# An mLSTM cell feeding a quick-GELU layer: the second chunk's gates computed later, one batch's mask moved to GpSimd, ScalarE's conversion steps separated, and the loads put in another order

## The chip, the core and the metric

The kernel runs on one core of one Trainium2 chip. The metric is the device time of one execution in microseconds, the median of several runs; less is better. Five runs of the kernel before gave 485.58, 485.70, 485.89, 485.89 and 486.21 us.

A core has engines that run beside each other, each on its own list of instructions in a fixed order: TensorE (PE in the profile; its weight loads are shown as PEld), VectorE (DVE), ScalarE (ACT), GpSimd (POOL), and SyncE (SP), which here only issues DMAs. An instruction starts when the one before it on its engine has gone ahead and the semaphores it waits for have come.

## What is computed

Two layers, one behind the other. The first is a recurrent cell over 768 steps for 4 batches of 8 heads, head size 40; the second multiplies each of the 3072 rows of 320 numbers by a 320 x 2048 matrix, applies a quick GELU, and multiplies by a 2048 x 320 matrix.

```python
for t in range(S):
    m_new = np.maximum(f_gate[:, :, t] + m, i_gate[:, :, t])
    f_stab = np.exp(f_gate[:, :, t] + m - m_new)
    i_stab = np.exp(i_gate[:, :, t] - m_new)
    m = m_new
    C = f_stab[..., None, None] * C + i_stab[..., None, None] * np.einsum('bhd,bhe->bhde', vt, kt)
    n = f_stab[..., None] * n + i_stab[..., None] * kt
    h_tilde = np.einsum('bhde,bhe->bhd', C, qt)
    denom = np.maximum(np.abs(np.einsum('bhd,bhd->bh', n, qt)[:, :, None]), 1.0)
    y[:, :, t] = 1.0 / (1.0 + np.exp(-o_gate[:, :, t])) * h_tilde / denom
...
h = x @ w_in
out = (h * (1.0 / (1.0 + np.exp(-1.702 * h)))) @ w_out
```

## The kernel before

The 768 steps are cut into six chunks (`w` = 0 to 5) of 128 steps. Within a chunk the recurrence becomes an attention: scores k times q (`scores`, L350), multiplied on VectorE by a matrix of decay weights that is zero above the diagonal (`weights`, then L352), times v (`values`, L362), divided and gated on VectorE (`y`, L389 to L395), transposed (`seam`, L404 on TensorE, L405 on ScalarE) and given to the up projection, the GELU and the down projection. What a chunk hands on is a state per head.

The gates of a chunk are two scans and six short operations on VectorE (`gates`, L254 to L281), on 32 partitions (one per batch and head). The running maximum `m_run` is also written to DRAM as a row (L269), from where `spread` (L316) reads it back, broadcast over 128 partitions, as the raw material of the next chunk's weights. For chunks from 1 on, ScalarE turns these into weights with eight activations per batch (L334), and GpSimd sets what lies above the diagonal to zero (L336). Chunk 0 has no time for the way through DRAM: there TensorE builds the exponents in PSUM from bf16 parts (L328, L329). A first matmul (L324) puts -1e30 above the diagonal, so that ScalarE's exponential (L330) gives zero there.

The weights of both projections come from DRAM in twenty pieces of 512 KB: 0 to 9 are `w_in`, 10 to 19 are `w_out`. `fetch` issues the loads, `convert` turns a piece into the form that TensorE uses: two ScalarE steps (L228 on the high words into the destination, L229 on the low words in place) and four VectorE steps (L232, L233, L235, L237), of which only L237 reads what L229 wrote. Six pieces fit into the tile `big`, and a slot is free again when its piece has been converted: piece 10 takes the slot of piece 0, and so on.

There is no scheduler: each engine's order is the order in which the program writes the calls (`manual_schedule`). SyncE issues nearly all DMAs in one order as well: at the start gates, keys and queries (`"kq"`), values and output gates (`"vo"`) by batch, and the weight pieces in between. An issue that has to wait holds what follows. For chunk 1 the keys and queries are also loaded as blocks of 32 steps (`load_blocks`, 16 DMAs each for `k_bl` and `q_bl`, L117), which VectorE transposes (L301). PSUM has eight tiles; `ps_a` has four of them in turn, so a matmul may also wait until an earlier reader of its tile is done.

Chunk 0 starts with a list written out by hand (L683 to L740). Then comes the loop over chunks: `up` or `up_fast`, then the down projection in blocks. In chunk 0 the function `weights_in(n)` places the conversions between the stages from a table `beside`, with the fetches that go with each; the pieces of the next chunk's attention (`side`) are put between the down blocks.

Of the kernel before, what the change touches and what calls it, by code (L numbers as in the profile page):

```python
# [12 lines left out]
OP = mybir.AluOpType  # L13
# [9 lines left out]
L = 128  # L23
# [11 lines left out]
def kernel(  # L35
# [13 lines left out]
    B, H, S, D = q.shape  # L49
# [4 lines left out]
    NP = H // 2  # L54
# [20 lines left out]
    V, A, G, T = nc.vector, nc.scalar, nc.gpsimd, nc.tensor  # L75
# [91 lines left out]


    load_gates(0)
    for what, n in (("kq", 0), ("kq", 1), (load_gates, 1), ("vo", 0), ("vo", 1), ("kq", 2), (fetch, 0), ("kq", 3),  # L170
                    (fetch, 1), ("vo", 2), ("vo", 3), *((fetch, n) for n in range(2, 10))):
        if isinstance(what, str):
            load(0, what, slice(n, n + 1))
        else:
            what(n)
# [5 lines left out]
    not_yet, ident_bf = (xs.bitcast(BF)[:, i * L:(i + 1) * L] for i in range(2))  # L181
# [21 lines left out]
    for t in (k_st, q_st):  # L203
# [16 lines left out]
    kT, qT, wt, ys, xT, gs, o_ps, p_c = {}, {}, {}, {}, {}, {}, {}, {}  # L220


    def convert(n, engines="AV"):

        lo, hi, dst = bits[n][:, :, 0], bits[n][:, :, 1], pieces[n][0]
        dst_u = dst.bitcast(U32)
        if "A" in engines:
            A.activation(out=dst, in_=hi.bitcast(FP), func=AF.Abs)  # L228
            A.activation(out=lo, in_=lo, func=AF.Copy, scale=2.0 ** -29)  # L229
        if "V" not in engines:  # L230
# [81 lines left out]
    def spread(w):  # L312

        for b in range(B):
            x = wt[w, b] = work.tile([L, NP, 2, L], FP, tag="wt", bufs=4, name="wt")
            nc.sync.dma_start(out=x.rearrange("s p i t -> s (p i) t"),  # L316
                              in_=m_row[w][b * H:(b + 1) * H, :].unsqueeze(0).to_broadcast([L, H, L]))

    def weights(w, b):
        if w == 0:  # L320
            x = wt[w, b] = work.tile([L, NP, 2, L], FP, tag="wt", bufs=4, name="wt")
            for i in range(2):
                pw = ps_a.tile([L, NP, L], FP, tag="a", name="p_w")
                T.matmul(pw, ident_bf, not_yet.unsqueeze(1).to_broadcast([L, NP, L]), start=True, stop=False)  # L324
                for p in range(NP):
                    h = b * H + 2 * p + i
                    one = pick[:, h:h + 1].to_broadcast([3 * BH, L])
                    T.matmul(pw[:, p, :], one, m3, start=False, stop=False)  # L328
                    T.matmul(pw[:, p, :], a3, one, start=False, stop=(p == NP - 1))  # L329
                A.activation(out=x[:, :, i, :], in_=pw, func=AF.Exp)  # L330
            return
        x = wt[w, b].rearrange("s p i t -> s (p i) t")
        for h in range(H):
            A.activation(out=x[:, h, :], in_=x[:, h, :], func=AF.Exp, scale=-1.0,  # L334
                         bias=cols[w][:, b * H + h:b * H + h + 1])
        G.affine_select(out=x, in_=x, compare_op=OP.is_ge, fill=0.0, base=0, pattern=[[0, H], [1, L]],  # L336
                        channel_multiplier=-1)
        if w > 1 and b == 0:
            gates_out(w)

# [342 lines left out]
    transposes(0, 0)  # L683
    weights(0, 0)
    transposes(0, 1)
    gates(1)
    scores(0, 0)
    weights(0, 1)
    scores(0, 1)
# [2 lines left out]
    values(0, 0)  # L692
    values(0, 1)
    transposes(0, 2)
    convert(0, "A")
    weights(0, 2)
    seam(0, 0)
    seam(0, 1)
    convert(0, "V")
    scores(0, 2)  # L700
    convert(1, "A")
    transposes(0, 3)
    weights(0, 3)
    convert(1, "V")
    scores(0, 3)
# [17 lines left out]
    values(0, 3, states=True)  # L723
    full_rows(0, 0, 0)
    full_rows(1, 0, 0)
    convert(2, "A")
    seam(0, 2)
    full_rows(0, 1, 0)
    seam(0, 3)
# [7 lines left out]
    for j in range(2):  # L737
        for i in range(2):
# [2 lines left out]

    beside = {0: ((5,), range(10, 15)), 1: ((6, 7, 8), ()), 2: ((9, 10, 11), (16,)), 3: ((12, 13, 14), (18, 19)),
              4: ((15,), ()), 8: ((16,), ()), 10: ((17,), ()), 12: ((18,), ()), 14: ((19,), ())}

    def weights_in(n):
        done, ahead = beside.get(n, ((), ()))
        for p in done:
            convert(p)  # L750
        for p in ahead:
            fetch(p)

# [7 lines left out]
    for w in range(NW):  # L761
        more = w + 1 < NW
        for j in range(NF // 2):
# [10 lines left out]
                up_fast(w, j, next_keys if more and j == 0 else None)  # L774
            if w == 0 and j == 0:
                load_blocks(1, 0)
                fetch(15)
                spread(1)
                load_blocks(1, 1)
            if w == 1 and j == 3:  # L780
                weight_sums(3)
            if more:
# [87 lines left out]
```

## Time and profile before

| what | value |
|---|---|
| median of five runs | 485.89 us (485.58 to 486.21) |
| the profiled execution's own time | 485.58 us |
| its span in the profile | 483.9 us |
| TensorE busy / weight loads busy | 478.0 us / 396.9 us |
| VectorE, ScalarE, GpSimd busy | 342.3, 220.9, 60.3 us |
| TensorE's granted clock | 1.00 over the span |
| DMA, mean over the span | 93 GB/s |
| DMA, second to fourth 12 us of the span | 210, 280, 286 GB/s |

The profile covers one execution; its span is a little shorter than the time, which also holds what lies before the first and after the last instruction. In lists of instructions the columns are start in us, duration in us, engine, line and operation, what it writes and reads, the count of instructions merged into the row, and in brackets how long the engine was idle before it and what ended the idle time. In the table of stretches each engine has its busy time and, in brackets, its number of instructions; behind them stand the granted clock, the busy share of the DMA engines and the GB/s.

### The profile page before, as it was taken

Reading aid. Unit: us, or ns where it says so; the run is one execution under the profiler, and the core shown is the slowest. Engines: PE = TensorE matmul, PEld = TensorE weight load, DVE = VectorE, ACT = ScalarE, POOL = GpSimd, SP = SyncE. Lnnn points to the kernel's source line nnn. Section 1 sums busy time; section 2 is a strip of 40 time slices with the busy share of each in tenths; the row PEclk is TensorE's granted clock in tenths of the full one; section 3 lists DMA queues with packets and bytes.
Section 4 is the critical chain, followed back from the end, with each engine's and each line's share of the span. In section 5 each row is a group of like instructions: output and inputs, shape, how many; then the busy total and the mean of one; then the engine's idle time right before and its main releaser. Section 6 shows DMA issues by size and latency. Waiting matters only on the chain. (4 is left out here: it accounts for less than half of the span.)

```text
span 483.9 us, 10433 instructions
## 1 busy us (share of the span) xinstructions
PE 478.0 (99%) x4072; PEld 396.9 (82%) x4072; DVE 342.3 (71%) x853; ACT 220.9 (46%) x575; POOL 60.3 (12%) x101
## 2 busy tenths in 40 slices
PE   8999999999999999999999999999999999999997
PEld 5874467777779999788999877999877999977997
DVE  8788888887978965667766677686576786254831
ACT  7667675403649302468600466900374920255300
POOL 3020001520001420000341000332000120000000
PEclk9999999999999999999999999999999999999999
DMA  9999779944997000997000896200492000000000
GB/s 127 210 280 286 165 140 235 133 65 72 193 177 79 6 30 28 218 152 81 3 29 15 126 249 65 28 28 3 85 261 21 1 15 16 28 1 0 1 34 22
DMA packets 176097, 44.87 MB, mean 93 GB/s; under 512 B 164368, under 2 KB 169648, under 8 KB 176048
## 3 DMA queue, kind: packets, MB, share of 16 engines
q1 hardware_dynamic: 175472, 43.55, 48.9%
q8 instruction: 32, 0.52, 0.5%
q10 hardware_dynamic: 576, 0.66, 0.4%
q14 instruction: 17, 0.14, 0.1%
HBM read 40.17 MB, written 4.01 MB: 91 GB/s over the span
## 5 line engine op out<-in xcount | busy, mean ns | idle before, releaser
L615 PE MATMUL p_out<-w_out_sb,g 128*128 128x160 f32 x480 | 69.8, 301 | 0.0
L615 PEld LDWEIGHTS p_out<-w_out_sb,g 128*128 128x128 f32 x480 | 66.3, 190 | 0.9
L405 ACT COPY xT<-p_x 128x384 f32<-128x384 f32 x24 | 10.8, 483 | 122.1 <-PE p_x L404 109.0
L526 DVE TENSOR_TENSOR g<-p_u,g 128x256 f32<-128x256 f32 x80 | 33.7, 424 | 44.6 <-PE p_u L518 35.0
L523 ACT COPY g<-p_u 128x256 f32<-128x256 f32 x120 | 43.1, 377 | 43.5 <-PE p_u L518 39.3
L530 ACT ACTIVATE g<-g 128x256 f32<-128x256 f32 x120 | 42.3, 425 | 39.3 <-DVE g L526 39.3
L336 POOL TENSOR_SCALAR_AFFINE_SELECT wt<-wt 128x1024 f32<-128x1024 f32 x20 | 22.7, 1137 | 238.0 <-ACT wt L334 208.1
L620 DVE TENSOR_TENSOR o_sb<-o_sb,p_out 128x160 f32<-128x160 f32 x70 | 21.4, 317 | 42.2 <-PE p_out L615 41.8
L334 ACT ACTIVATE wt<-wt,cols 128x128 f32<-128x128 f32 x160 | 47.8, 391 | 0.0
L518 PE MATMUL p_u<-xT,w_in_sb 128*128 128x256 f32 x160 | 38.9, 382 | 0.0
L518 PE MATMUL p_u<-xs,big 128*128 128x256 f32 x160 | 37.9, 379 | 0.0
L546 PE MATMUL p_v<-xT,w_in_x 64*128 64x512 f32 x80 | 37.0, 602 | 0.0
L546 PE MATMUL p_u<-xT,w_in_x 64*128 64x512 f32 x80 | 37.0, 602 | 0.0
L352 DVE TENSOR_TENSOR wt<-p_s,wt 128x512 f32<-128x512 f32 x48 | 30.4, 682 | 8.5 <-POOL wt L336 6.7
L566 PE MATMUL p_out<-w_out_sb,g 128*128 128x320 f32 x128 | 36.3, 436 | 0.0
L615 PE MATMUL p_out<-t,big 128*128 128x160 f32 x240 | 35.5, 301 | 0.0
L518 PEld LDWEIGHTS p_u<-xT,w_in_sb 128*128 128x128 f32 x160 | 29.6, 190 | 5.4 <-DVE o_sb L620 1.5
L518 PEld LDWEIGHTS p_u<-xs,big 128*128 128x128 f32 x160 | 30.0, 190 | 4.6 <-ACT g L523 0.2
L615 PEld LDWEIGHTS p_out<-t,big 128*128 128x128 f32 x240 | 33.3, 190 | 0.2
L566 PEld LDWEIGHTS p_out<-w_out_sb,g 128*128 128x128 f32 x128 | 23.8, 190 | 9.8 <-issue 0.5
L526 DVE TENSOR_TENSOR g<-p_v,g 128x256 f32<-128x256 f32 x80 | 29.8, 414 | 0.0
L546 PEld LDWEIGHTS p_v<-xT,w_in_x 64*128 64x128 f32 x80 | 14.2, 186 | 16.0 <-issue 16.0
(172 smaller groups left out, 857.3 us busy)
## 6 DMA issues: line engine op xcount, KB each, us to landing
wt<-m_row SPq DMA_DIRECT2D x20, 512.0 KB, 7.0
v_st<-in_v_dram SPq DMA_DIRECT2D x5, 640.0 KB, 8.8
eo<-in_o_gate_dram SPq DMA_DIRECT2D x5, 640.0 KB, 5.6
k_st<-in_k_dram SPq DMA_DIRECT2D x5, 640.0 KB, 11.2
out_dram<-o_sb SPq DMA_DIRECT2D x19, 160.0 KB, 1.8
big<-in_moe_w_in_dram SPq DMA_DIRECT2D x5, 512.0 KB, 6.6
k_bl<-in_k_dram SPq DMA_DIRECT2D x40, 64.0 KB, 2.7
q_bl<-in_q_dram SPq DMA_DIRECT2D x40, 64.0 KB, 2.6
```

The lines of the kernel that those rows point to most:

```text
L334: A.activation(out=x[:, h, :], in_=x[:, h, :], func=AF.Exp, scale=-1.0, bias=cols[w][:, b * H + h:b * H + h + 1])
L336: G.affine_select(out=x, in_=x, compare_op=OP.is_ge, fill=0.0, base=0, pattern=[[0, H], [1, L]], channel_multiplier=-1)
L352: V.tensor_tensor(out=wt[w, b][:, :, i, :], in0=pw[i], in1=wt[w, b][:, :, i, :], op=OP.mult)
L405: A.copy(out=xT[w][:, :, b, :], in_=px)
L518: T.matmul(p[k][:, ts[t]], a[:, k // 2, k % 2 * 128:(k % 2 + 1) * 128], b, start=first, stop=True, skip_group_check=True)
L523: A.copy(out=g[k][i][:, ts[t]], in_=chain[k][:, ts[0]])
L526: V.tensor_tensor(out=g[k][i][:, ts[t]], in0=p[k][:, ts[pt]], in1=g[k][i][:, ts[t]], op=OP.add)
L530: A.activation(out=dst, in_=dst if src is None else src, func=AF.Gelu_apprx_sigmoid)
L546: T.matmul(p[k], w_in_x[r, k, :], x[r, 2, :], start=False, stop=True, skip_group_check=True)
L566: T.matmul(po, gs[w, f // 2][:, f % 2, b * L:(b + 1) * L], w_out_sb[:, f, :], start=(f == 0), stop=(f == NF - 1))
L615: T.matmul(po, a(f), b[:, f, :], start=(f == 0), stop=(f == NH - 1))
L620: V.tensor_tensor(out=dst, in0=x, in1=po, op=OP.add)
```

## The change

Six edits, all of which concern chunk 0 and the material for chunk 1.

1. The loads of chunk 1's gates are issued behind the ten pieces of `w_in`, not behind the keys and queries of batch 1.
2. `gates(1)` leaves the list at the start, where it stood between the transposes of batch 1 and the scores of batch 0. It is called when piece 9 has been converted.
3. For batch 1 of chunk 0 the -1e30 matmul is left out (two instructions with their weight loads), and GpSimd sets the values above the diagonal to zero after the exponential, once for each half of the heads.
4. `convert` takes its ScalarE steps apart, "H" and "L". For piece 0, "L" comes behind the weights of batch 2; for piece 1, behind the transposes of batch 3.
5. In SyncE's order the blocks of keys come behind pieces 10 and 11, and the blocks of queries behind pieces 12 to 15. Before, keys stood behind pieces 10 to 14, and queries behind piece 15 and the broadcast.
6. The row's way through DRAM follows the gates: written behind the queries' blocks, read back (`spread(1)`) behind piece 16.

```diff
-    for what, n in (("kq", 0), ("kq", 1), (load_gates, 1), ("vo", 0), ("vo", 1), ("kq", 2), (fetch, 0), ("kq", 3),
-                    (fetch, 1), ("vo", 2), ("vo", 3), *((fetch, n) for n in range(2, 10))):
+    for what, n in (("kq", 0), ("kq", 1), ("vo", 0), ("vo", 1), ("kq", 2), (fetch, 0), ("kq", 3),
+                    (fetch, 1), ("vo", 2), ("vo", 3), *((fetch, n) for n in range(2, 10)), (load_gates, 1)):
...
-    def convert(n, engines="AV"):
+    def convert(n, steps="HLV"):
...
-        if "A" in engines:
+        if "H" in steps:
             A.activation(out=dst, in_=hi.bitcast(FP), func=AF.Abs)
+        if "L" in steps:
             A.activation(out=lo, in_=lo, func=AF.Copy, scale=2.0 ** -29)
...
+    def causal(x, n):
+
+        G.affine_select(out=x, in_=x, compare_op=OP.is_ge, fill=0.0, base=0, pattern=[[0, n], [1, L]],
+                        channel_multiplier=-1)
+
     def weights(w, b):
         if w == 0:
...
-                T.matmul(pw, ident_bf, not_yet.unsqueeze(1).to_broadcast([L, NP, L]), start=True, stop=False)
+                if b != 1:
+                    T.matmul(pw, ident_bf, not_yet.unsqueeze(1).to_broadcast([L, NP, L]), start=True, stop=False)
...
-                    T.matmul(pw[:, p, :], one, m3, start=False, stop=False)
-                    T.matmul(pw[:, p, :], a3, one, start=False, stop=(p == NP - 1))
+                    T.matmul(pw[:, p, :], one, m3, start=(b == 1), stop=False)
+                    T.matmul(pw[:, p, :], a3, one, start=False, stop=(b == 1 or p == NP - 1))
                 A.activation(out=x[:, :, i, :], in_=pw, func=AF.Exp)
+                if b == 1:
+                    causal(x[:, :, i, :], NP)
...
     transposes(0, 1)
-    gates(1)
     scores(0, 0)
...
-    convert(0, "A")
+    convert(0, "H")
     weights(0, 2)
+    convert(0, "L")
     seam(0, 0)
     seam(0, 1)
     convert(0, "V")
     scores(0, 2)
-    convert(1, "A")
+    convert(1, "H")
     transposes(0, 3)
+    convert(1, "L")
     weights(0, 3)
...
-    beside = {0: ((5,), range(10, 15)), 1: ((6, 7, 8), ()), 2: ((9, 10, 11), (16,)), 3: ((12, 13, 14), (18, 19)),
+    beside = {0: ((5,), (10, 11)), 1: ((6, 7, 8), ()), 2: ((9, 10, 11), (16,)), 3: ((12, 13, 14), (18, 19)),
...
             convert(p)
+            if p == 9:
+                gates(1)
...
             if w == 0 and j == 0:
                 load_blocks(1, 0)
-                fetch(15)
+                for n in range(12, 16):
+                    fetch(n)
+                load_blocks(1, 1)
+            if w == 0 and j == 4:
                 spread(1)
-                load_blocks(1, 1)
```

More of the change, by code (lines that the diff above doesn't have):

```diff
@@ L220 @@
     kT, qT, wt, ys, xT, gs, o_ps, p_c = {}, {}, {}, {}, {}, {}, {}, {}
-    def convert(n, engines="AV"):
+    def convert(n, steps="HLV"):
         lo, hi, dst = bits[n][:, :, 0], bits[n][:, :, 1], pieces[n][0]
         dst_u = dst.bitcast(U32)
-        if "A" in engines:
+        if "H" in steps:
             A.activation(out=dst, in_=hi.bitcast(FP), func=AF.Abs)
+        if "L" in steps:
             A.activation(out=lo, in_=lo, func=AF.Copy, scale=2.0 ** -29)
-        if "V" not in engines:
+        if "V" not in steps:
             return
@@ L335, in weights @@
                          bias=cols[w][:, b * H + h:b * H + h + 1])
-        G.affine_select(out=x, in_=x, compare_op=OP.is_ge, fill=0.0, base=0, pattern=[[0, H], [1, L]],
-                        channel_multiplier=-1)
+        causal(x, H)
         if w > 1 and b == 0:
@@ L725 @@
     full_rows(1, 0, 0)
-    convert(2, "A")
+    convert(2, "HL")
     seam(0, 2)
```

## The prediction

> **What bounds the kernel now.** I read the row of busy shares first, then the table by stretches of time, then VectorE's and TensorE's timelines of the first 30 us, then those of 50 to 85 us, where the moved work lands.
>
> ```profile
> PE 478.0 (99%) x4072; PEld 396.9 (82%) x4072; DVE 342.3 (71%) x853; ACT 220.9 (46%) x575; POOL 60.3 (12%) x101
> ...
> 8.00:26.50 18.50, 17.91 (x282) 15.24 (x279) 15.26 (x39) 12.14 (x26) 2.14 (x5) 1.00 1.18 210
> 26.50:36.20 9.70, 9.70 (x52) 7.21 (x48) 8.56 (x18) 6.51 (x11) 1.76 (x4) 1.00 1.02 279
> 36.20:66.50 30.30, 30.30 (x145) 13.69 (x144) 24.09 (x45) 20.66 (x37) 0.16 (x1) 1.00 0.84 224
> ```
>
> TensorE is busy 99%, at a granted clock of 1.00. A modelled end can hide a stall, so I checked its pace: 16 matmuls of the up stage take 7.13 us both at 43.15 and at 52.13, and 16 of L566 4.57 us at 85.50, 91.98 and 104.61. From 26.56 us on TensorE simply has work. A microsecond is won there only by less TensorE work, or by reaching 26.56 earlier, and then it stays won to the end. The start is different:
>
> ```profile
> 8.63 0.41 DVE L254 TENSOR_TENSOR_SCAN f_run<-one,fi 32x128 f32<-32x128 f32 x1 [0.48 <-DMA fi<-in_f_gate_dram]
> ...
> 10.82 0.22 DVE L281 TENSOR_SCALAR dec_in<-pair,both 32x16 f32<-32x16 f32 x1
> 10.97 1.27 DVE L352 TENSOR_TENSOR wt<-p_s,wt 128x512 f32<-128x512 f32 x2
> 13.35 1.29 DVE L352 TENSOR_TENSOR wt<-p_s,wt 128x512 f32<-128x512 f32 x2 [1.11 <-PE p_s L350]
> ...
> 12.29 0.96 PEld L350 LDWEIGHTS p_s<-qT,kT 40*128 40x128 f32 x14 [0.30 <-DVE wt L352]
> ...
> 19.08 0.29 PEld L350 LDWEIGHTS p_s<-qT,kT 40*128 40x128 f32 x2 [0.60 <-ACT wt L330]
> ...
> 25.62 0.90 PEld L362 LDWEIGHTS p_o<-v_st,wt 128*64 128x64 f32 x28 [0.15 <-DVE wt L352]
> ```
>
> VectorE starts the first scores' product (L352) at 10.97, right behind the eight instructions of gates(1) (8.63 to 11.04), though TensorE's scores ended at 9.08 + 1.16 = 10.24. TensorE then waits for L352 (11.69, 12.29), at 19.08 for ScalarE's L330, and at 25.62 again for VectorE.
>
> **The change, part by part.**
>
> *gates(1) out of the start.* L352 began 0.09 to 0.10 us before the modelled end of its scores at 13.35 and 20.63, so it can start at 10.14 instead of 10.97: **-0.83 us**. TensorE's second half of the next scores, held until the second L352 ended (12.24), starts near 11.46 and ends at 12.61 instead of 13.44: the 0.83 stays.
>
> *No mask matmul for batch 1.* Two matmuls L324, worth 0.23 and 0.21 us by the start of the next instruction (10.17 to 10.40, 10.85 to 11.06), leave TensorE. Without them TensorE is ready for the scores at 11.25, just before VectorE lets it go; with them it would be ready at 11.69 and eat 0.23 of the 0.83. They are part of that gain, not an addition.
>
> *Two masks on GpSimd, 128x512 each.* No such row. Nearest are 0.29 us for 128x128 (the start) and 1.09 for 128x1024 (L336); a line through them gives 0.65. Bounds: 0.55 (half of L336) and 1.09 each. ScalarE's two L330 would end at about 11.44 and 12.07, so the masks end at 12.16 and 12.81; the two L352 that need them start at 12.52 and 13.16. Hidden, with 0.35 to spare; at 1.09 each the second ends at 13.69 and costs 0.53.
>
> A rule speaks against this part. The Trainium skill, "SBUF — State Buffer", section "Who interferes with whom", has a VectorE instruction with two SBUF inputs and a GpSimd instruction that reads SBUF block each other for whole instructions. The trace agrees where the form fits: L494 (both inputs in SBUF) took 2.00 us at 72.03 beside the mask at 71.44, 1.18 us without it. But L352 reads its first input from PSUM:
>
> ```profile
> 158.90 1.09 POOL L336 TENSOR_SCALAR_AFFINE_SELECT wt<-wt 128x1024 f32<-128x1024 f32 x1 [1.25 <-ACT wt L334]
> ...
> 158.86 1.28 DVE L352 TENSOR_TENSOR wt<-p_s,wt 128x512 f32<-128x512 f32 x2
> ```
>
> Side by side, both keep their usual time. Were the lock to hold here, L352 would wait for 12.81 instead of 12.52: +0.29. I take the row: 0.
>
> *ScalarE's parts split.* L228 and L229 of piece 0 (17.29, 17.86) precede L330 (18.44), for which TensorE waits at 19.08. With L229 behind L330, L330 ends about 0.58 earlier, on top of the 0.83; these scores end near 19.3, no longer late. VectorE is then free at 20.44 - 0.83 = 19.61, and its 0.18 us wait before 20.63 goes: **-1.02** at the third batch's L352. L229 now ends at 18.88, its reader L237 starts at 18.92: hidden, barely. In the second split TensorE's transposes hold ScalarE's copies anyway: nothing.
>
> *What holds this back: loads.* Piece 1 of the weights was issued at 13.07 and landed after 7.2 us, at 20.27; its L228 ran at 20.30. If it lands no earlier, VectorE's conversion of piece 1 starts at 20.98 instead of 20.82 and the gain is 0.86. SyncE no longer issues two gate loads (4.57 to 5.81, 1.2 us) ahead of it, but the loads there land at a pace of 1.0 to 1.1 us each, so only some tenths can follow. Between 0.86 and 1.02 I take **-0.95**. The wait at 25.62 shows that TensorE passes this on.
>
> *gates(1) in its new place* follows piece 9's conversion on VectorE, near 50.1 us (51.08 - 0.95). Its eight instructions took 2.41 us from 8.63 to 11.04. Behind it wait the conversions of pieces 10 to 15. VectorE idled 1.26 us at 57.05 and 1.84 us at 66.04 for ScalarE, so piece 14 ends 2.41 - 1.26 = 1.15 late, at 64.40, and piece 15 on time. TensorE needs piece 14 first for f = 6, at 67.06 + 4 x 0.267 - 0.95 = 67.2. Cost 0; without those two pauses 2.41 would still fit into the 3.9 us by which piece 14 was early.
>
> *SyncE's queue.* Before: pieces 10 to 14 (to 42.62), keys' blocks (11.0 us), piece 15, the broadcast of m_row (54.73), queries' blocks (14.1 us, to 71.1), piece 16. After, from about 28.5: pieces 10 and 11 (2), keys (11.0), pieces 12 to 15 (4), queries (14.1), m_row (0.6) end near 60.2. Piece 12, issued near 42, lands after some 5 us, and ScalarE wants it at 55.4. Piece 16 comes about 10 us earlier and ends ScalarE's 1.60 us wait at 75.30, which TensorE never felt: 0.
>
> The broadcast becomes late: it waits for gates(1)'s row to land. Row: 1.4 us median for m_row; behind the queries' blocks 2.5 (their own landing). "DMA: Bandwidth & Descriptors", section on the anatomy of one DMA, puts a fixed part of about 2.0 us on any DMA, for GpSimd's path. By either the broadcast starts at 62.2 to 62.7, and its first batch lands between 2.5 us (512 KB alone, piece 16) and 6.3 us (its own row) later: 65.2 to 69.0, when ScalarE wants it at 67.98. I take 69.0, the same operation. Cover: ScalarE's wait of 1.60 behind those 16 activations, 0.37 until VectorE takes piece 16, and 1.1 (0.52 before L352 at 79.27, 0.59 until TensorE's values at 82.34), together 3.0. So the landing may come at 71.0; later, each microsecond costs one.
>
> **Sum.** -0.95. The profiled execution took 485.58 us for a span of 483.9; it becomes 484.63 and 482.95. It was the fastest of the five, so I forecast the median: 485.89 - 0.95 = 484.94.
>
> **Rivals.** (a) *As counted*: gain 0.7 to 1.2, 484.7 to 485.2. For it: each wait is a row. Against: it passes through four places with slack below 0.4 us. Chance 0.62. (b) *Loads come forward too*: if piece 1 and the v and o loads land the full 1.2 us sooner, loads stop nothing. TensorE waits 1.76 us in this stretch (0.59 and 0.18 before 14.7, 0.84 around 19.1, 0.15 at 25.6), and 0.44 us of matmuls goes; 1.5 of these 2.2 would give 484.4. Chance 0.12. (c) *GpSimd's masks become the wait*: at 1.09 us each they eat 0.53: 485.5. L336's smooth row speaks against. Chance 0.09. (d) *The broadcast is the bound*, the slower side: if keys' and queries' small blocks hold SyncE (single issues stalled 3.6 us at 61.7 before), the row of weights comes late, ScalarE's 16 activations hold piece 16, then L352, then TensorE at 82. From a landing at 71.0 it costs; from 72.0 it has eaten the gain; 73.5 gives 487.4. For it: issues of 2.9 us (13.07) and 3.9 us (73.14) show that SyncE stalls when much is queued, and keys' blocks now follow seven weight pieces. Against: 2 us of cover left by my slow estimate. Chance 0.12. Other delays of pieces 12 to 14: 0.05, slower. That gates(1) doesn't leave the start can't be: the instruction order shows it behind piece 9.
>
> **Numbers.** 0.2% is 0.97 us, about what a measurement of this kernel can tell from no change, and the forecast stands on that line: I split (a) 0.34 faster, 0.28 same. Faster 0.34 + 0.12 = 0.46; same 0.28 + 0.09 = 0.37; slower 0.17. The range reaches from 484.2 (b) to 486.6, which takes in (c) and the milder half of (d).
>
> **What would show it.** The first L352 near 10.1 us; the wait before 19.08 gone; the third batch's L352 near 19.6; the first full matmuls (26.56 before) near 25.6; masks of 0.65 us; ScalarE's 16 activations starting near 69, with TensorE at its old pace from 60 to 110. I am wrong if L352 waits for GpSimd, if piece 1 lands later than 20.3, or if TensorE idles near 82.

## The result, and the profile after

The changed kernel takes 488.70 us in the median of 23 runs (485.64 to 493.75); the kernel before takes 485.83 beside it. The ratio is 1.0052, with a 95% interval of 1.0039 to 1.0065: slower. Its fastest run, 485.64, only equals the fastest one before, 485.58, so even the best execution shows no gain.

The scatter is part of the result. Of 24 executions with a clock on record two, over 493 us, are set apart as slow; of the 22 others, 10 show a mean granted clock of 0.986 to 0.997 and take 488.1 to 491.9 us; the other 12 show 0.999 or 1.000 and take 485.6 to 488.7. The profiled execution took 491.35 us for a span of 489.6, with a mean clock of 0.997.

First the rows of busy shares and of the granted clock on the page of the changed kernel:

```profile
PE 480.4 (98%) x4070; PEld 399.0 (81%) x4070; DVE 341.8 (70%) x853; ACT 221.0 (45%) x575; POOL 61.4 (13%) x103
...
PEclk9999999899999999999999999999999999999999
```

TensorE has two matmuls fewer and is still busy for 2.4 us longer, and one slice of the clock's row falls to 8. The eighth slice is 86 to 98 us. What happens ahead of it stands in the timelines of ScalarE, VectorE and TensorE (the new line numbers: L334 is now L343, L352 is L360, L362 is L370, L566 is L574):

```profile
76.67 4.78 ACT L343 ACTIVATE wt<-wt,cols 128x128 f32<-128x128 f32 x16 [7.17 <-DMA wt<-m_row]
81.35 0.66 ACT L228 ACTIVATE w_out_sb<-big 128x512 f32<-128x512 f32 x1
...
82.04 0.84 DVE L233 TENSOR_SCALAR w_out_sb<-w_out_sb 128x512 f32<-128x512 f32 x1 [5.91 <-ACT w_out_sb L228]
84.93 2.48 DVE L360 TENSOR_TENSOR wt<-p_s,wt 128x512 f32<-128x512 f32 x4
...
85.67 0.32 PE L370 MATMUL p_o<-v_st,wt 128*64 128x41 f32 x4 [2.82 <-DVE wt L360]
86.36 2.73 PE L370 MATMUL p_o<-v_st,wt 128*64 128x41 f32 x60 [0.37 <-ACT w_out_sb L228]
```

This is one chain through three engines. The broadcast row lands near 76.6, and until then ScalarE stands for 7.17 us. Its 16 activations (4.78 us) hold the conversion of piece 16 that is queued behind them; VectorE has stood 5.91 us for that conversion, and its L360 is queued behind it in turn; TensorE, out of other work, stands 2.82 and 0.37 us for L360. From the row's landing to TensorE's values it is 85.67 - 76.67 = 9.0 us.

The pause has a second price. The table of stretches, behind the pause (the third number from the end is the granted clock):

```profile
86.00:88.00 2.00, 1.57 (x45) 1.51 (x46) 1.97 (x5) 2.00 (x7) 0.00 (x0) 0.95 1.35 204
88.00:90.00 2.00, 2.00 (x38) 2.00 (x37) 1.59 (x3) 1.88 (x6) 0.76 (x1) 0.50 0.82 206
90.00:92.00 2.00, 2.00 (x23) 1.66 (x20) 1.60 (x6) 0.91 (x2) 0.72 (x1) 0.69 0.80 200
```

The clock falls to one half and comes back to 1.00 in 92 to 94 us: 2 x (0.05 + 0.50 + 0.31) = 1.72 us of TensorE's work are lost.

The whole difference of the spans, 489.6 - 483.9 = 5.7 us, can be counted at three points. The hidden layer's first full matmuls (L719, now L728) begin at 27.01 in place of 26.56: +0.45. The values begin at 85.67 in place of 82.34: another +2.88. The down projection behind them resumes at 91.25 in place of 85.50: another +2.42, of which 1.7 is the clock and 0.37 the second stand. Together 5.75; behind that point the two traces run alike.

Why the row is late stands in SyncE's own list:

```profile
30.41 0.54 SPq L97 DMA_DIRECT2D fi<-in_f_gate_dram  x1
31.75 0.33 SPq L97 DMA_DIRECT2D fi<-in_i_gate_dram  x1
33.71 6.71 SPq L166 DMA_DIRECT2D big<-in_moe_w_out_dram  x5
42.59 8.72 SPq L117 DMA_DIRECT2D k_bl<-in_k_dram  x16
51.41 5.25 SPq L166 DMA_DIRECT2D big<-in_moe_w_out_dram  x9
56.75 11.72 SPq L117 DMA_DIRECT2D q_bl<-in_q_dram  x16
68.57 0.43 SPq L270 DMA_DIRECT2D m_row<-m_run  x1
69.10 1.32 SPq L166 DMA_DIRECT2D big<-in_moe_w_out_dram  x3
70.86 1.75 SPq L317 DMA_DIRECT2D wt<-m_row  x4
```

In the kernel before, the same stretch of the list is:

```profile
30.18 12.40 SPq L166 DMA_DIRECT2D big<-in_moe_w_out_dram  x12
42.62 11.01 SPq L117 DMA_DIRECT2D k_bl<-in_k_dram  x16
```

The keys' blocks begin at 42.59 in place of 42.62, although 5 DMAs of weights stand ahead of them in place of 12 (pieces 12 to 14 are gone), and two gate loads in place of the row's write. The issues at 30 to 42 us are not held up by their own cost: the DMAs take eight semaphores in turn, so the ninth waits until the first has landed. In the kernel before, the issues at 40.68 and 41.18 come 0.02 us behind the landings (40.66, 41.16) of DMAs issued at 30.18 and 31.44. In the changed kernel the first block of keys, at 42.59, comes 0.01 us behind the landing (42.58) of the last piece of `w_in`, issued at 29.42. Taking DMAs out of that stretch brings the rest forward only as far as the landings allow. With the order alone changed (g2 below) the keys begin at 37.37; here that gain is gone, because the last piece of `w_in` landed 4 us later than before (38.55).

### The profile page after: what moved, and what is told of

It is laid out like the page before. It is cut to its first block, busy times and chain, and to the rows that moved or that the text cites. A ratio compares the mean times of both kernels' runs of the same rounds, so it can differ in the third digit from the quotient of the medians.

```text
span 489.6 us, 10425 instructions
## 1 busy us (share of the span) xinstructions
PE 480.4 (98%) x4070; PEld 399.0 (81%) x4070; DVE 341.8 (70%) x853; ACT 221.0 (45%) x575; POOL 61.4 (13%) x103
## 5 line engine op out<-in xcount | busy, mean ns | idle before, releaser
L322 POOL TENSOR_SCALAR_AFFINE_SELECT wt<-wt 128x1024 f32<-128x1024 f32 (+1 forms) x22 | 23.8, 1085 | 247.7 <-ACT wt L343 243.0
L343 ACT ACTIVATE wt<-wt,cols 128x128 f32<-128x128 f32 x160 | 47.8, 391 | 7.2 <-DMA wt<-m_row 7.2
L360 DVE TENSOR_TENSOR wt<-p_s,wt 128x512 f32<-128x512 f32 x48 | 30.4, 682 | 10.5 <-POOL wt L322 6.7
L574 PE MATMUL p_out<-w_out_sb,g 128*128 128x320 f32 x128 | 36.3, 436 | 0.0
L574 PEld LDWEIGHTS p_out<-w_out_sb,g 128*128 128x128 f32 x128 | 23.8, 190 | 9.9 <-issue 0.7
L370 PE MATMUL p_o<-v_st,wt 128*64 128x41 f32 x768 | 26.9, 232 | 3.6 <-DVE wt L360 2.8
L370 PEld LDWEIGHTS p_o<-v_st,wt 128*64 128x64 f32 x768 | 24.7, 140 | 6.6 <-DVE wt L360 3.7
```

What stands on the lines that cost most here:

```text
L360: V.tensor_tensor(out=wt[w, b][:, :, i, :], in0=pw[i], in1=wt[w, b][:, :, i, :], op=OP.mult)
L370: T.matmul(po[b][t, h, :], wt[w, b][:, p, i, t], v_st[:, b * H + h, :], start=True, stop=True)
L574: T.matmul(po, gs[w, f // 2][:, f % 2, b * L:(b + 1) * L], w_out_sb[:, f, :], start=(f == 0), stop=(f == NF - 1))
```

## The experiments

There are eighteen runs, each beside runs of the kernel before on the same chip: fifteen variants, one of them twice, and the changed kernel and the kernel before once more. They are told in four groups.

### Which part of the queue's new order costs

**e0**: the changed kernel unaltered, for a second profile.

> The changed kernel unaltered, beside the variants below. Theory (the broadcast of the second chunk's row is issued behind the queries' 16 DMAs and lands late): ScalarE waits for wt<-m_row again, some 7 us ahead of the first L343, TensorE stands some 3 us near 82 to 86 us, and the time is 487 to 490, ratio 1.003 to 1.007 to before. Rival (chance of one profiled execution, in which the loads of pieces 10 and 11 landed late): no such wait here, and a time near 485.8.

Measured: 487.74 us (11 runs), ratio 1.0043 (1.0022 to 1.0065). ScalarE gets the row at 75.52 after a wait of 6.00, TensorE stands 1.65 and 0.37 us, and the clock is 0.83, 0.50 and 0.82 in 84 to 90 us. No accident of one profile.

**e1**: only the queries' blocks go behind the broadcast again.

```diff
-                load_blocks(1, 1)
             if w == 0 and j == 4:
                 spread(1)
+                load_blocks(1, 1)
```

> All of the change is kept but one place: the queries' 16 block DMAs are issued behind the row's broadcast instead of ahead of it. Theory (the queries' blocks in SP's queue make the broadcast late): the broadcast is issued some 11 to 12 us earlier, near 59 to 60 us, lands by 66 to 67; no DMA wait at L343, no TensorE wait near 82 us, and the time falls to 485.0 to 486.3, equal to before within 0.2%. Rival 1 (the gates computed late, with the row written to and read from HBM behind pieces 12 to 16, are late by themselves): still a wait of 2 us or more at L343 and 487 or more. Rival 2 (the loss is at the start or in the granted clock, unrelated to the broadcast): unchanged, 487 to 490.

Measured: 487.21 us, ratio 1.0036 (1.0025 to 1.0048). The wait at L343 is gone, and the time is not. In VectorE's and TensorE's timelines of e1:

```profile
77.47 2.49 DVE L302 STREAM_TRANSPOSE qT<-q_bl 128x512 f32<-128x512 f32 x4 [2.93 <-DMA q_bl<-in_q_dram]
...
83.75 2.21 PE L370 MATMUL p_o<-v_st,wt 128*64 128x41 f32 x60 [0.38 <-DVE wt L360]
```

Now the queries' blocks are late: VectorE stands 2.93 us for them (in the kernel before it began these transposes at 73.94 without a wait), and from the start of the hidden layer to the down projection behind the values e1 takes 59.98 us (27.08 to 87.06) where the kernel before takes 58.94 (26.56 to 85.50). None of the three theories had this. SyncE's list in e1 shows where it comes from. The keys' blocks are all issued by 48.76, earlier than before (53.63). But between them and the broadcast now stand pieces 12 to 15, the row's write, piece 16 and the wait for the row's landing, so the broadcast is issued at 58.67 in place of 54.73 and the queries' blocks from 60.84 on in place of 56.95. Either order leaves one of the two late.

**e2**: the gates go back to the start, with their loads and the row's write; the rest of the change stays.

```diff
+("kq", 0), ("kq", 1), (load_gates, 1), ("vo", 0), ...
+    gates(1)
     scores(0, 0)
...
-            if p == 9:
-                gates(1)
```

> The late gates are undone: the second chunk's gates are loaded and computed at the start as before, its row is written early; masks, ScalarE's split and the new order of SP's queue (keys behind two pieces, queries behind six, broadcast behind both) stay. Theory (SP's order alone makes the broadcast late): the wait at L343 stays, shorter by the row's own write (issued 68.57, broadcast 70.86, so 1 to 2 us of 7.2), time 486.5 to 489. Rival 1 (late gates are the cause): the wait is gone and the time is that of before, 485.8.

Measured: 486.73 us, ratio 1.0018 (1.0006 to 1.0030). The wait at L343 is 4.42 us, until 73.71, and TensorE stands 0.37 us: on the edge. The first theory holds. The row's late write costs somewhat more than the 1 to 2 us it named: ScalarE gets the row 1.8 to 3.0 us earlier than in the profiles where it is written behind the queries (75.52, 76.10 in g1 below, 76.67).

**f1**: the converse. The start's edits stay and the row is written before the keys, pieces 10 to 14 are ahead of the keys as before, and only the queries are ahead of the broadcast.

```diff
                 fetch(15)
-                spread(1)
                 load_blocks(1, 1)
+                spread(1)
```

> The start's edits as in e3, pieces and keys in the order of the kernel before, but the queries' 16 block DMAs ahead of the row's broadcast: of the change's new order of SP's queue this is the one part that e1 takes back. Theory (the broadcast behind the queries is late by itself): issued near 68 to 71, a wait of ScalarE at L339 of 3 to 6 us, TensorE stands near 83 us for 0 to 2 us, time 486.5 to 488.5. Rival (the keys ahead of pieces 12 to 14 make everything behind them late, and the broadcast's place alone costs nothing, since the values of the second batch leave it some 5 us): L339 waits, but TensorE does not stand at 83 us, time that of e3, 486.1.

Measured: 486.22 us, ratio 1.0009 (1.0003 to 1.0016), the same as e3 below, which has the other order. The rival is right:

```profile
71.55 4.79 ACT L339 ACTIVATE wt<-wt,cols 128x128 f32<-128x128 f32 x16 [1.79 <-DMA wt<-m_row]
...
83.05 2.07 PE L367 MATMUL p_o<-v_st,wt 128*64 128x41 f32 x64
```

The row is 1.79 us late for ScalarE, and TensorE begins its values without a wait.

**g1**: the changed kernel, with pieces 12 to 14 back ahead of the keys.

```diff
-    beside = {0: ((5,), (10, 11)), ...
+    beside = {0: ((5,), range(10, 15)), ...
...
-                for n in range(12, 16):
-                    fetch(n)
+                fetch(15)
```

> The changed kernel with one part taken back: pieces 12 to 14 are issued ahead of the keys' blocks again, as before; late gates, queries ahead of the row, row behind piece 16, masks and split stay. Theory (keys ahead of pieces 12 to 14 are what makes all behind them late, since SP then issues the inefficient block DMAs while the first weights still land and the pieces afterwards): broadcast lands 2 to 3 us earlier than in the changed kernel (near 73 to 74, a wait of 2 to 5 us at L343), TensorE stands under 0.5 us near 83 us, time 486.0 to 486.8. Rival (the row written late, behind the queries, is what costs): a stand of 1 us or more near 83 us and 487 or more.

Measured: 487.20 us, ratio 1.0027 (1.0016 to 1.0038). My theory of the keys falls:

```profile
76.10 4.78 ACT L343 ACTIVATE wt<-wt,cols 128x128 f32<-128x128 f32 x16 [6.93 <-DMA wt<-m_row]
...
85.11 0.32 PE L370 MATMUL p_o<-v_st,wt 128*64 128x41 f32 x4 [2.58 <-DVE wt L360]
```

From f1 to g1 two gate loads come ahead of piece 10, the row is written behind the queries, and piece 16 is put ahead of the broadcast. The broadcast is issued at 69.12 in place of 66.19 and ScalarE gets its first batch after 7.0 us in place of 5.4: 4.6 us later in all. That is what takes the row past its cover. Which of the three edits has which share is not taken apart.

**g2** and **k0**: the two order edits, each alone in the kernel before. g2 puts the keys behind two pieces and pieces 12 to 15 behind the keys; k0 swaps `spread(1)` and `load_blocks(1, 1)`, as in f1's diff.

> The kernel before with one part of the change alone: the keys' blocks behind pieces 10 and 11, pieces 12 to 15 behind the keys; gates, masks, conversions and the broadcast ahead of the queries as before. Theory (the keys' place costs): the queries' blocks land 2 to 3 us later, VectorE waits 1 to 3 us for them at the transposes near 74 to 77, TensorE stands 0 to 0.6 us near 83, time 486.0 to 486.8. Rival (in e1 the hole of the start alone made the queue late): 485.7 to 486.0, no wait for the queries.

> The kernel before with only the queries' blocks put ahead of the row's broadcast. Theory (this edit alone has more room than the other order, since the second batch's values want the row some 5 us later than the queries' transposes want the queries): the row lands near 70 to 71, a wait under 2 us at ScalarE, no stand of TensorE near 83, and executions in which the start's loads are late lose less: median 485.6 to 485.8, fewer runs above 486.2. Rival (the row's lateness reaches TensorE): 486.2 or more.

Measured: 485.69 (ratio 0.9999, 0.9991 to 1.0007) and 485.67 (0.9999, 0.9991 to 1.0007). g2's theory falls, k0's holds: neither edit costs anything alone, and in k0 the row lands at 68.08, before ScalarE comes to it at 69.03. All 13 runs of k0 lie below 486.2. SyncE's list in g2 shows what moving seven DMAs of weights brings by itself:

```profile
37.37 11.04 SPq L117 DMA_DIRECT2D k_bl<-in_k_dram  x16
```

The keys begin 5.25 us earlier than in the kernel before, 0.02 us behind the landing (37.35) of the load eight places ahead.

The profiles with a late row agree on one number, the time from ScalarE's first activation to TensorE's values: 76.67 to 85.67, 75.52 to 84.53, 76.10 to 85.11, 73.71 to 82.72, each 9.0 us. In the changed kernel TensorE was ready for the values at 82.34 + 0.45 = 82.79, so, for a start as late as this one, the row could come until 73.8. f1 (71.55) is inside, e2 (73.71) on the edge, g1, e0 and the first profile outside.

### Where the start's gain went

**e3**: the start's edits alone (late gates, behind pieces 10 to 14; masks; split), SyncE's order as before. **b0**: the kernel before, profiled a second time. **a1**, **a2**, **a3**: masks, split and late gates each alone in the kernel before.

> The start's edits alone: gates computed late (in the first place where the hidden layer's weights are converted), ScalarE's parts split, masks of the second batch by GpSimd; loads of the second chunk's gates and the whole order of SP's queue for pieces, blocks and broadcast as before. Theory 1 (the start is limited by when pieces 0 and 1 land, since ScalarE's converting of piece 0 stands in order ahead of the third batch's L337): the first L360 comes 0.5 to 0.8 us earlier, but the resumed hidden layer starts within 0.3 us of before's 26.56, time 485.3 to 486.0. Rival (the start's 0.83 to 1.02 us of the prediction come true once the broadcast is not late): PE's L728 at 25.6 to 25.8, time 484.8 to 485.1. Either way no DMA wait at L343.

> The kernel before, unaltered, profiled a second time. Theory (one or more of the start's edits bring the hole in the DMA engines' work near 16.5 to 18 us, in which SP's issue of piece 1 stands 3.7 to 4.7 us): here the issue stands about 2.9 us again, piece 0 lands near 16.2, piece 1 near 20.3, no hole, the hidden layer resumes near 26.6. Rival (the hole comes by chance in any kernel): a longer stand, piece 1 near 21 to 22, and a time above 486.5 in such executions.

> Of the change only the second batch's masks by GpSimd in place of the two L324. If the prediction's step holds: the two masks hidden, TensorE 0.44 us shorter there but bounded by VectorE's gates, time within 0.1 us of before, 485.7 to 485.9. If this edit brings the hole in the loads: piece 1 lands at 21 or later and the time is 486.0 to 486.5, scattered.

> Of the change only the split of ScalarE's converting parts. Prediction's step: L330 of the third batch begins one part (0.57 us) earlier, third batch's L352 up to 0.6 us earlier, time 484.8 to 485.5 if TensorE there waits for ScalarE and not for piece 0. Rival (piece 0's landing holds ScalarE all the same): 485.7 to 486.0. If this edit brings the hole: 486.0 to 486.5.

> Of the change only gates(1) late (to the first place of the hidden layer's weights), its loads as before. Prediction's step: first L352 at 10.1 to 10.5 in place of 10.97, the second at 12.5 to 12.7 in place of 13.35, and the gain carried to the hidden layer: 485.0 to 485.2. Rival (what follows waits for pieces 0 and 1 through ScalarE, so an earlier third batch only waits longer): 485.6 to 486.1, with a longer wait at L330 of the third batch; a wait of 1.2 us or more on TensorE there also brings a clock of 0.5 to 0.8 in the 4 us behind it, worth 1.7 us, in some executions.

Measured:

| kernel | median us | ratio and interval |
|---|---|---|
| e3, all three | 486.11 | 1.0014 (1.0004 to 1.0025) |
| b0, before again | 485.76 | 0.9997 (0.9984 to 1.0010) |
| a1, masks | 486.56 | 1.0022 (1.0009 to 1.0036) |
| a2, split | 485.56 | 0.9998 (0.9987 to 1.0009) |
| a3, late gates | 486.30 | 1.0011 (1.0003 to 1.0018) |

No part gives what the prediction took for all together. Of the expectations, b0's theory holds (its issue of piece 1 stands 2.98 us), a3's rival holds at a little more than its time, and a1 took the branch of the late loads; e3 (486.11, the hidden layer at 28.85 with a lowered clock) fits neither of its two, and a2 lies between its two. The changed kernel's start shows why. From VectorE's, GpSimd's and ScalarE's timelines:

```profile
10.50 1.29 DVE L360 TENSOR_TENSOR wt<-p_s,wt 128x512 f32<-128x512 f32 x2 [2.34 <-PE p_s L358]
12.69 1.29 DVE L360 TENSOR_TENSOR wt<-p_s,wt 128x512 f32<-128x512 f32 x2 [0.91 <-PE p_s L358]
...
11.72 1.22 POOL L322 TENSOR_SCALAR_AFFINE_SELECT wt<-wt 128x512 f32<-128x512 f32 x2 [4.74 <-ACT wt L337]
...
17.40 0.68 ACT L228 ACTIVATE w_in_sb<-big 128x512 f32<-128x512 f32 x1 [0.65 <-DMA big<-in_moe_w_in_dram]
17.98 1.06 ACT L337 ACTIVATE wt<-p_w 128x512 f32<-128x512 f32 x2
21.09 0.69 ACT L228 ACTIVATE w_in_sb<-big 128x512 f32<-128x512 f32 x1 [0.73 <-DMA big<-in_moe_w_in_dram]
...
18.11 0.43 DVE L233 TENSOR_SCALAR w_in_sb<-w_in_sb 128x512 f32<-128x512 f32 x1 [1.33 <-ACT w_in_sb L228]
```

The first product is 0.47 us earlier (10.97 before), the second 0.66 (13.35), and the masks are hidden. Then both engines meet piece 0: ScalarE waits 0.65 us for it with the third batch's L337 queued behind, VectorE 1.33 us (0.56 before). The time that was saved is spent waiting for a load, and the loads have become later: piece 0 landed at 17.38 (16.22 before), piece 1 at 21.06 (20.28). In the seven profiles with late gates (the changed kernel, e0, e1, a3, f1, g1, k2; e3, with a lowered clock, and c1 apart) the hidden layer begins 5.9 to 6.1 us behind the landing of piece 1. Piece 1 sets it, not the gates.

Why the load is late could only be followed for one step. At piece 1, SyncE's issue stands for as long as the table says:

| kernel | issue of piece 1 stands, us | piece 1 lands | hidden layer begins |
|---|---|---|---|
| before; again; p1; g2; k0 | 2.94; 2.98; 2.93; 3.00; 2.89 | 20.11 to 20.48 | 26.56 to 26.80 |
| split alone: a2; k1; k1 again | 3.70; 2.67; 3.51 | 20.87; 20.34; 20.72 | 26.40; 26.37; 26.27 |
| late gates: a3; with split, k2 | 3.64; 3.92 | 20.75; 21.13 | 26.84; 27.07 |
| late gates, masks, split: changed; e0; e1; g1; f1 | 3.71; 3.69; 3.86; 3.50; 4.08 | 20.76 to 21.36 | 26.69 to 27.28 |
| the same three, e3 | 4.70 | 22.03 | 28.85 |
| masks: a1; with split, e2 | 4.59; 4.05 | 21.90; 21.28 | 28.95; 26.81 |

While it stands, and until its first data come, the DMA engines run nearly dry. The view of the DMA queues, busy tenths in 40 slices of 12 to 19 us, of the kernel before and of e3:

```profile
DMA  9999999998877999999999999999998989899999
...
DMA  9999999997989899999999999998311110000089
```

From 16.9 to 18.6 us the second moves 25 GB/s, the kernel before 251. All kernels with late gates or masks show the longer stand (c1 below too, 3.77), and of those with neither only two of the three profiles with the split (c2 below, 2.63). How an edit on VectorE or GpSimd reaches SyncE's queue stays open; the order of the DMAs up to piece 9 in e2, e3, a1 and a3 is that of the kernel before. The lateness grows along the queue: the last piece of `w_in` lands at 38.45 to 39.93 us in the seven profiles with an issue of 3.0 us or less (before, b0, p1, g2, k0, k1, c2), and at 40.36 to 43.35 in the thirteen others.

**c1** and **c2**: if the attention should not stand behind a load, put `convert(0)` and `convert(1)` behind the scores of the third and the fourth batch. c1 has late gates besides (not in the diff), c2 not.

```diff
-    convert(0, "A")
     weights(0, 2)
     seam(0, 0)
     seam(0, 1)
-    convert(0, "V")
     scores(0, 2)
-    convert(1, "A")
+    convert(0)
     transposes(0, 3)
     weights(0, 3)
-    convert(1, "V")
     scores(0, 3)
     columns(0)
+    convert(1)
```

> The kernel before, with gates(1) late as in a3 and, besides, the converting of pieces 0 and 1 put behind the third and the fourth batch's scores, so that no part of the attention stands in order behind a load. Theory (in the changed kernel the start's gain ends at piece 0's landing, because ScalarE's L330 and VectorE's L352 of the third batch stand behind the converting of piece 0): third batch's L352 near 18.2 to 18.8 in place of 20.63, VectorE's 7.3 us of converting and L352 end near 25.4, the hidden layer resumes near 25.5 in place of 26.56, time 484.7 to 485.2. Rival (VectorE is full from 18 us on, and the order in it does not matter): 26.3 to 26.8 and 485.6 to 486.0. If the loads' hole comes, piece 1 lands near 21 to 22, still ahead of its converting.

> Only the converting of pieces 0 and 1 put behind the third and fourth batch's scores; gates where the kernel before has them. Theory: third batch's L352 near 18.9 to 19.5, hidden layer 0.3 to 0.7 us earlier than 26.56, time 485.1 to 485.6. Rival: no gain or 0.5 us later, since VectorE idles until the third batch's scores are there, 485.8 to 486.4.

Measured: 486.89 (1.0025, 1.0015 to 1.0034) and 487.31 (1.0032, 1.0019 to 1.0044). The hidden layer begins early, as the theories said (25.65 and 25.82), but the time falls outside theory and rival alike. TensorE's timeline of c1:

```profile
25.65 1.99 PE L716 MATMUL p_h<-xT,w_in_sb 128*128 128x256 f32 x8
29.21 0.63 PE L404 MATMUL p_x<-ident,y 128*128 128x128 f32 x3 [1.56 <-DVE y L395]
```

The hidden layer begins 0.91 us earlier than in the kernel before, and 3.6 us later TensorE gives it back with interest: the `y` of the last batches now come behind the conversion of piece 1 on VectorE. The row of L566 at 79.99 in the kernel before stands at 81.34 here. VectorE was idle for 2.50 us before the third batch's L352, which came at 19.67 and not at 18.2 to 18.8, because its scores were not there; from 20 to 30 us it is busy 9.34 of 10 us (9.19 in the kernel before), so what is put off there is not made up. A milestone in the middle says nothing about the end. Both kernels scatter little (c1's 10 runs 486.79 to 487.37), which would fit a scatter that comes from ScalarE's wait for the pieces; no run tests this.

### Does a pause of TensorE lower the clock

**p1**: the kernel before, with four pauses in the last chunk, made by 1, 4, 8 and 14 small memsets on GpSimd between two idle matmuls, which change nothing in the output.

```diff
+            if not more and i in (1, 4, 7, 10):
...
+                T.matmul(p_stop[:, 0:128], idle, idle, start=True, stop=True)
+                for _ in range({1: 1, 4: 4, 7: 8, 10: 14}[i]):
+                    G.memset(idle, 0.0)
+                T.matmul(p_stop[:, 0:128], idle, idle, start=True, stop=True)
```

> The kernel before, with four pauses put on TensorE in the last chunk, where it is busy throughout: it waits for 1, 4, 8 and 14 small memsets of GpSimd, some 0.3 to 4 us. Theory (a pause of TensorE over some 1.2 us is followed by about 4 to 6 us at a lower granted clock, worth about 1.7 us, and a shorter one is not): granted clock 1.00 behind the short pauses, 0.5 to 0.8 behind those over 1.3 us, and the time rises by the pauses' sum plus 1.7 us for each long one. Rival (the lower clock near 86 to 92 us and 20 to 26 us in the other profiles had another cause, such as the load on the chip there): clock 1.00 throughout, the time rises by the pauses' sum alone.

Measured: 497.74 us (496.39 to 498.35). The pauses were 0.33, 1.17, 2.22 and 3.79 us:

```profile
461.12 0.23 PE L815 MATMUL p_stop<-idle 128*128 128x128 bf16 x1 [1.17 <-POOL idle L814]
470.20 0.23 PE L815 MATMUL p_stop<-idle 128*128 128x128 bf16 x1 [2.22 <-POOL idle L814]
480.85 0.29 PE L815 MATMUL p_stop<-idle 128*128 128x128 bf16 x1 [3.79 <-POOL idle L814]
...
470.00:472.00 2.00, 1.80 (x14) 1.80 (x15) 0.00 (x0) 0.00 (x0) 0.14 (x1) 1.00 0.00 0
482.00:484.00 2.00, 2.00 (x10) 2.00 (x9) 0.00 (x0) 0.00 (x0) 0.00 (x0) 0.50 0.00 0
```

A pause alone does bring the lower clock, so the rival falls; but a threshold of 1.2 us falls too. The waits sum to 7.5 us and the clock's loss to about 3.0 (0.50 from 480.85 to 486.84), of the 11.8 by which the span grew; the rest, 1.3 us, was not followed. The pause of 2.22 us left the clock at 1.00 here, the one of 3.79 brought 0.50 for some 6 us. In other profiles shorter ones were enough: 1.28 us at 19.31 in e3 and 1.36 at 19.83 in a1 were each followed by a clock of 0.50 in 22 to 24 us, while 0.80 us at 83.05 in a2 was not.

How long the half clock lasts is the same throughout: 87.82 to 91.23 in the changed kernel, and 3.41 us as well in e0, g1, a1 and e3; in p1 it is twice that, 480.02 to 486.84.

The Trainium skill, "TensorE: Matmul & The Clock Gate", part 1, fits most of this: the clock is either full or half, decided over free-running windows of about 3.4 us. Half of 3.41 is 1.7 us, the 1.72 counted above, and a free-running window would explain why one execution loses it and the next does not. Its condition, at least one idle window, does not fit: the pauses of 1.28 to 2.82 us were shorter than a window, and here the measurement decides. In the 3.41 us ahead of the half clock TensorE was still busy for 1.71 us in the changed kernel and for 2.13 in e3. How much of a window must be idle stays open: in p1 the stretch from 466.37 to 469.78, with 1.61 us busy, was followed by the full clock.

### A version below both

k0 showed that the queries ahead of the broadcast cost nothing and are all issued by 62.70 in place of 71.08; a2's split starts the hidden layer 0.16 us earlier, but a2's profile lost 0.80 and 0.37 us near 83 us, because VectorE waited 2.78 us, until 76.64, for the loads of the queries' transposes. **k1** has both; **k2** adds the late gates.

> The kernel before with ScalarE's split and the queries ahead of the row's broadcast: what a2 and f1 point to. Theory: the hidden layer resumes 0.16 to 0.3 us earlier as in a2, the stand near 83 us that a2 showed (0.80 and 0.37) is gone, median 485.2 to 485.5, below before. Rival (the split's gain is lost again to the loads): 485.6 to 486.0.

> The kernel of k1 (ScalarE's split, and the queries ahead of the row) a second time, for the size of its gain. Theory: median 485.2 to 485.5, at most one run above 486.2, ratio 0.9990 to 0.9996. Rival (k1's runs were lucky): as before, 485.7, with a tail to 487.

> The kernel of k1 and, besides, gates(1) late as in a3 (its loads early, the row written behind pieces 10 to 14). Theory 1 (the late gates only turn VectorE's work into waiting for piece 0, and the start's loads land later with them): SP's issue of piece 1 stands 3.5 us or more, the hidden layer resumes at 26.6 to 27.1, median 485.7 to 486.3. Rival (the late stands at the start came by chance, and with the split the 2.41 us of VectorE do pay): an issue of 2.6 to 3.0 us, the hidden layer at 26.0 or earlier, 484.8 to 485.2.

Measured: k1 485.39 (0.9993, 0.9985 to 1.0001), the second time 485.43 (485.28 to 485.90) beside 485.77, ratio 0.9990 (0.9982 to 0.9999). All 26 runs of k1 lie at 485.9 or below, while a2's reached 487.94. TensorE's row in the profile of the second time:

```profile
26.27 1.99 PE L722 MATMUL p_h<-xT,w_in_sb 128*128 128x256 f32 x8
```

The issue of piece 1 stood 3.51 us in it, the row came 1.63 us late for ScalarE, and the time was still good. The gain, 0.3 us or 0.1%, is small: the first interval includes no change, the second only just does not. k2 took 486.12 (1.0009, 1.0001 to 1.0018): its issue of piece 1 stood 3.92 us, its hidden layer began at 27.07, and its first theory holds.

## Why the prediction was wrong, point by point

**The bound.** "A microsecond is won there only by less TensorE work, or by reaching 26.56 earlier" was half of the truth: a microsecond is also lost there by a wait, and the profile after shows 3.2 us of it at 82 us and 1.7 us of clock behind it.

**gates(1) out of the start, -0.83.** Half right in size. The first product came at 10.50 and not at 10.14: its scores began at 9.23 in place of 9.08, and it began 0.11 us behind their modelled end where the sum had it 0.10 ahead. The second came 0.66 us earlier. This stayed to 13.9 us (0.66 by the row behind the second product) and was gone at 18.

**Masks.** Right as a row: 0.61 us each by the merged row, where 0.65 was taken, hidden. L360, which ran beside the second mask for 0.25 us, kept its 1.29 us; the rule about the lock that the prediction cites names two SBUF inputs, and L360 has one. As an edit, a1 was slower by 0.2%, with later loads in its profile, which the prediction had no term for.

**ScalarE's split, -1.02 at the third batch.** Wrong for the changed kernel: its third batch's L360 began at 20.47, not at 19.61. The step let VectorE arrive earlier at this product, but `convert(0, "V")` stands ahead of it in VectorE's list, and this begins when piece 0 has landed and gone through ScalarE. By the lines of the kernel before this would have held: piece 0 landed at 16.22 there, and L228 would have come to it at 17.29 - 0.83 = 16.46. In the changed kernel it landed at 17.38, and VectorE's conversion began at 18.11 in place of 18.00. Alone, the split gave the little it can: 26.27 to 26.40 in place of 26.56.

**Loads, "only some tenths can follow".** Wrong in sign. Pieces 0 and 1 landed 1.2 and 0.8 us later, the third batch's keys and queries landed within 0.07 us of where they had, and "if it lands no earlier", which bounded the gain at 0.86 from below, was no bound: it could land later. That piece 1 later than 20.3 would make it wrong was the right sign to name.

**gates(1) in its new place, 0.** No run shows a cost of VectorE's 2.41 us there; what it cost was the row's later write.

**SyncE's queue, the step that failed.** "After, from about 28.5: pieces 10 and 11 (2), keys (11.0), pieces 12 to 15 (4), queries (14.1), m_row (0.6) end near 60.2." Its durations were right enough: from the first block of keys to the row's write 26.0 us went by, where the sum has 29.7. Its beginning was wrong: the keys came at 42.59 where the sum has 30.5, 12.1 us late. The sum gave pieces 10 and 11 two microseconds, the time of their issues, but this stretch of the queue is paced by landings: a DMA goes out when the one eight places ahead has landed. Of the 12.1 us, 6.9 stand in g2 too (37.37), where only the order was changed. The other 5.2 are one DMA more ahead of the keys (two gate loads for one write of the row), 1.3 us in g2's landings, and the last piece of `w_in`, which landed at 42.58 in place of g2's 38.63; why the loads were late stays open. Against 60.2 the row was written at 68.57, the broadcast issued at 70.86 against 62.2 to 62.7, and landed near 76.6 against 69.0. The last leg was right: 5.7 us from issue to landing, with 6.3 taken.

**The cover, 3.0 us.** Too small, in the safe direction: the row may land until 73.8, not 71.0, as the constant 9.0 us shows (with TensorE ready 0.45 us later than before, where the sum had it 0.95 earlier). "Later, each microsecond costs one" held: 76.67 - 73.8 = 2.9, and TensorE came 2.88 late. It left out what a pause costs besides, 1.7 us of clock.

**Rivals.** (d), the broadcast as the bound, is what happened, by the path through ScalarE, piece 16 and L352 that it names; its chance of 0.12 was too small. Its size was off on both sides: with the cover as it was a landing at 73.5 would have cost nothing, and the real landing came 3 us later still. (c) did not happen, (b) was the opposite of what the loads did. The main case failed twice over, in the start's gain and in the queue.

## What to carry to other kernels

A queue with a fixed number of DMAs in flight is paced by landings while it is full: price a moved transfer by when the loads ahead of it land, not by adding up issues, and give the moved row the landing that follows from there. Cover is one account for all edits that draw on it: keys early cost nothing, queries ahead of the row cost nothing, and queries ahead of a row that is written late, with a piece ahead of its way back, overdrew it by 2 to 3 us, with the keys early (the changed kernel, e0) or not (g1). And before work is taken off an engine at a start that is fed by loads, look for the next load in that engine's own list: what is saved ahead of it turns into waiting.

## What the runs showed of the hardware that was not expected

- TensorE's clock after a pause: half clock for 3.41 us, worth 1.7 us, behind pauses of 1.28 to 2.82 us, and for some 6 us behind one of 3.79; none behind one of 2.22. It adds more than half to the price of the changed kernel's stand (1.7 us to 3.2), in some executions and not in others, and widens the scatter: the ten executions with a lowered clock took 488.1 to 491.9 us, the twelve others 485.6 to 488.7.
- The start's loads: with the same DMAs in the same order, an edit on other engines goes with an issue of piece 1 that stands 3.5 to 4.7 us in place of 2.6 to 3.0, and with DMA engines that run nearly dry meanwhile.
